# Three stages on one core: the gate's logits as 16 more columns of a product, weights decoded 768 words at a time

## The chip, the cores and the metric

The kernel runs on one core of a Trainium2 chip. The metric is the time of one execution on the device in microseconds (us); the median of three runs before the change is 947.0 us (946.34 to 947.67). The engines: TensorE (PE for its products, PEld for its weight loads), VectorE (DVE), ScalarE (ACT), GpSimd (POOL) and SyncE (SP), which issues nearly all DMAs. Each runs its own instructions in program order and waits for the others by semaphores.

## The reference, cut to what matters

```python
# 1. attention with decay: 4 batches, 8 heads, 768 steps, 48 wide; state is a 48x48 matrix per head
for t in range(S):
    y[:, :, t] = r_t @ (state + (u * k_t) outer v_t)
    state = w_t[:, None] * state + k_t outer v_t
x = y.transpose(0, 2, 1, 3).reshape(3072, 384)
# 2. gated feed-forward, weights given as float64 (384 x 1536, 384 x 1536, 1536 x 384)
xn = x / sqrt(mean(x * x) + 1e-6) * rms_g
x = (silu(xn @ w_gate) * (xn @ w_val)) @ w_out
# 3. eight experts, one per token (384 x 8 gates; 384 x 1024, 1024 x 384 per expert)
logits = x @ w_gate2;  e = argmax(logits);  p = softmax(logits)[e]
out = p * sigmoid(x @ w_output_gate)[e] * (relu(x @ w1[e]) @ w2[e])
```

## The kernel before, in words

The 3072 tokens are 24 tiles of 128 rows, and three tiles make a block of 384. Blocks 0 to 7 run one after the other. In each, TensorE computes the first product (function `l1`) for twelve slices f of 128 hidden columns, 18 matmuls of 384 columns per slice, and two slices later the second product (`l2`), 9 matmuls of 384 columns per slice. Every product is done in parts: an operand is split into a high part in the type fp32r and a low rest, and three products (high by high, high by low, low by high) replace one in full fp32 (`mm3`).

Between these matmuls stand slots, two in `l1` and one after `l2`, 36 and two more in a block. In a slot a table of offsets (`OFFS`, `TGAP`) advances the attention of the three tiles of the next block by a step, and `route` for the tiles of the block before. The attention of tiles 0 to 2 runs ahead of block 0, in an order written out by hand (`START_SEQ`: 0, 1, 2 advance that tile, 9 is a decode step, a negative number issues dummy matmuls). Then eight experts follow in units of 256 to 432 tokens.

Four places matter here.

- **Decoding.** The feed-forward weights arrive as float64 words of 8 bytes. `decode` takes a piece of 128 x 384 words: a load by SP, a conversion of the low half by ACT (line 100), a shift and a mask on DVE (lines 101 and 105), an integer addition on POOL (109), the high part by ACT (112) and the rest on DVE or, for every third piece, on POOL (115). There are 36 pieces. `decode_step` moves three pieces a stage on; the start calls it 8 times, every slot of block 0 once.
- **Scores.** For tiles from 6 on (`PARTED`, line 337) the scores are products in parts: ACT and DVE make high parts and rests of k and r (lines 369 to 400), and TensorE runs twelve matmuls of 256 columns (407). Tiles 0 to 5 use eight fp32 matmuls of 128 columns that contract over 48 rows, alternately in the lower and the upper half of the array (413).
- **Normalization.** Line 459 multiplies a tile of y by its row's factor and by `rms_g` on DVE; then TensorE transposes it (465), ACT takes the high part (467), DVE the rest (468).
- **Routing.** `route` transposes each tile of the feed-forward's result (534), copies it by ACT (538) and multiplies it by the 16 gate columns (527), a tile per step; then DVE finds the expert, TensorE counts places, and POOL scatters the rows to a scratch table in HBM. The last block is routed within the first unit of the first expert.

Buffers come from one ring of 18 slots, PSUM has three banks ("m") for attention, routing and transposes, two ("a") for `l1` and three ("l") for `l2`.

Of the kernel before, what the change touches and what calls it, by code (L numbers as in the profile page):

```python
# [9 lines left out]
F32 = mybir.dt.float32  # L10
# [12 lines left out]
def kernel(  # L23
# [15 lines left out]
    ROUTE_AT=(0, 1, 2, 3, 4),  # L39
    OFFS=((0, 0, 6.7, 7.5, 8.8, 10.5, 11.4, 11.5, 12.7), (0, 1.6, 3.2, 4.8, 6.4, 8, 9.6, 11.2, 12.8, 14.4)),  # L40
    TGAP=(8.9, 9.0),
    START_SEQ=(-11, 0, 0, 0, -4, -4, -6, -4, 0, 9, 1, 0, 1, 9, -4, 0, 1, 1, 2, -4, 0, 0, 1, 2, 0, 9, 1, -4, 2, 9, -6, 1, 2, 1, 2, 9, -4, 1, 2, 9, -2, 2, 2, 9, -6, 2, 9),
# [13 lines left out]
    ZC, LC, IC = DM, DM + 1, DM + 1 + E  # L56
    ROW = DM + 2 + E
# [13 lines left out]
    SLOT = -(-max(1536, SETW) // 8) * 8  # L71
# [3 lines left out]
    ring = ctx.enter_context(tc.tile_pool(name="ring", bufs=18))  # L75
# [4 lines left out]


# [6 lines left out]
    def decode(src, on_pool):  # L88
# [10 lines left out]
        ti, tf = t.bitcast(I32), t.bitcast(F32)  # L99
        nc.scalar.activation(out=low, in_=raw[:, :, 0], func=AF.Copy, scale=2.0 ** -29)  # L100
        nc.vector.tensor_scalar(
            t, raw[:, :, 1], 3, 0x3FFFFFF8, op0=ALU.logical_shift_left, op1=ALU.bitwise_and
# [3 lines left out]
            out=t, in0=raw[:, :, 1], scalar=0xC0000000, in1=t, op0=ALU.bitwise_and,  # L106
# [4 lines left out]
        hi, lo = src[2]()  # L111
        nc.scalar.activation(out=hi, in_=tf, func=AF.Copy)
        yield
# [16 lines left out]
    def split_rows2(raw):  # L130
        t = ring.tile([P, 2, 2 * DM], FR, tag="ring", name="rows2")
        split(raw.rearrange("p c n -> p (c n)"), t)
        return t.rearrange("p s (c n) -> p s c n", c=2)
# [9 lines left out]
    def split_w1(raw):  # L143
        t = ring.tile([P, 2, KD * 2 * P], FR, tag="ring", name="w1s")
        split(raw.rearrange("p c f -> p (c f)"), t)
        return t.rearrange("p s (c f) -> p s c f", c=KD)
# [7 lines left out]
    def ring_view(shape, dtype=F32):  # L154
        t = ring.tile([P, SLOT], dtype, tag="ring", name="rv")
        n = 1
        for x in shape:
            n *= x
        names = "abc"[:len(shape)]
        dims = " ".join(names)  # L160
        return t[:, 0:n].rearrange(f"p ({dims}) -> p {dims}", **dict(zip(names[1:], shape[1:])))


    def constants():
# [23 lines left out]
        c["g"] = const.tile([P, DM], F32, name="g_bc")  # L188
        nc.scalar.dma_start(out=c["g"], in_=rms_g.partition_broadcast(P))
        return c  # L190

    def route_constants(c, const):
# [3 lines left out]
        c["wr"] = const.tile([P, KD, 2 * E], F32, name="wr")  # L196
        nc.sync.dma_start(out=c["wr"], in_=w_gates)

# [62 lines left out]
    PARTED = 6  # L261
# [21 lines left out]
    def load_tile(i):  # L283
# [4 lines left out]
        if i == NSET:  # L288
            t = ring_view([SETW])
# [17 lines left out]
    def load_v(i):  # L307
# [3 lines left out]
        t = p3.tile([P, H, D], F32, tag="v", name="vt")  # L311
# [14 lines left out]
    def attention(c, i, xh, xl, col):  # L326
# [10 lines left out]
        parted = i >= PARTED  # L337
# [51 lines left out]
        if parted:  # L389
            rh, rl = wide  # L390
            kl = sc.tile([P, NPR, P], FR, tag="kl", name="kl")
            nc.vector.tensor_tensor(out=kl, in0=kq, in1=kh.bitcast(F32), op=ALU.subtract)
            for q in range(2):
                pr = slice(64 * q, 64 * q + 64)
                nc.scalar.activation(out=rh[pr, :, q], in_=rq[pr], func=AF.Copy)
            yield
            for q in range(2):
                pr = slice(64 * q, 64 * q + 64)
                nc.vector.tensor_tensor(
# [783 lines left out]
```

## Time and profile before

| | us |
|---|---|
| median of the runs (three) | 947.0 |
| the profiled execution | 944.41 |
| its span, from first to last instruction | 942.7 |
| PE busy, DVE busy, ACT busy, POOL busy | 890.2, 592.3, 326.3, 227.0 |
| mean granted clock of TensorE, 1 is full | 0.968 |

The profiled execution is 2.6 us under the median. A busy PE is not one at its peak: matmuls are pipelined, so a single one is shown as some 0.34 us while the next starts 0.175 us later. What a matmul costs is read from start to start. The span falls into a start (up to 49.6 us), block 0 (to 155.3), blocks 1 to 6 (to 621.0), block 7 (to 681.7) and the experts.

### The profile page before, as it was taken

To read this page: it belongs to the slowest core of one execution; us is meant where nothing else is said; L and a number is where in the kernel's file an instruction comes from. 1 tells how busy PE (TensorE), PEld (TensorE's weight loads), DVE (VectorE), ACT (ScalarE), POOL (GpSimd) and SP (SyncE) were. 2 spreads that over 40 slices of the span, in tenths; PEclk is the share of its full clock that TensorE was granted. 3 is DMA by queue.
4 is the path that set the end of the run, shared out by engine and by line. 5 is a ranking of instruction groups with operands and counts; after the bars stand their busy time and mean duration, and the time that the engine had idled before them with its cause. 6 is when DMAs were issued, how large, how long until landed. Compare 5 with 4: busy or idle time off the path is not lost. (4 is left out here: it accounts for less than half of the span.)

```text
span 942.7 us, 14866 instructions
## 1 busy us (share of the span) xinstructions
PE 890.2 (94%) x5579; PEld 864.3 (92%) x5579; DVE 592.3 (63%) x1147; ACT 326.3 (35%) x672; POOL 227.0 (24%) x326
## 2 busy tenths in 40 slices
PE   7786979999999999999999999999999999999995
PEld 4676979999999999999999998999999999999994
DVE  6899996764675586477367566624447565656551
ACT  1254344331332422333233232333434344434430
POOL 6666553212031031131113103201020100122111
PEclk8787799999999999999999999999999999999998
DMA  9445551761122121023012111101224363454510
GB/s 242 147 139 157 155 167 49 204 184 35 43 77 59 42 77 52 20 76 83 10 43 85 51 43 43 51 1 60 68 79 163 118 204 97 149 176 156 166 54 21
DMA packets 65142, 90.62 MB, mean 96 GB/s; under 512 B 5971, under 2 KB 55875, under 8 KB 65069
## 3 DMA queue, kind: packets, MB, share of 16 engines
q1 hardware_dynamic: 61213, 79.70, 28.7%
q0 software_dynamic: 3568, 9.57, 2.7%
q8 instruction: 44, 0.72, 0.3%
q10 hardware_dynamic: 288, 0.39, 0.1%
q14 instruction: 29, 0.24, 0.1%
HBM read 73.41 MB, written 16.73 MB: 96 GB/s over the span
## 5 line engine op out<-in xcount | busy, mean ns | idle before, releaser
L150 PE MATMUL a<-xh,gv 128*128 128x384 f32 x1152 | 325.7, 348 | 4.0 <-DVE sil L489 2.9
L150 PEld LDWEIGHTS a<-xh,gv 128*128 128x128 f32 x1152 | 215.9, 192 | 5.6 <-DVE sil L489 3.8
L150 PE MATMUL a<-xl,gv 128*128 128x384 f32 x576 | 197.5, 343 | 0.0
L489 DVE TENSOR_TENSOR sil<-a,sil 128x384 f32<-128x384 f32 x96 | 53.2, 554 | 112.5 <-PE a L150 110.6
L150 PE MATMUL a<-xh,w1s 128*128 128x256 f32 (+7 forms) x432 | 111.7, 324 | 1.5 <-DVE hl L868 1.2
L150 PEld LDWEIGHTS a<-xl,gv 128*128 128x128 f32 x576 | 111.0, 193 | 0.4 <-DVE xl L468 0.4
L491 ACT ACTIVATE hh<-sil 128x384 fp32r<-128x384 f32 x96 | 50.4, 525 | 163.1 <-DVE sil L489 163.1
L503 PE MATMUL l<-wo,hh 128*128 128x384 f32 x288 | 101.7, 353 | 0.0
L504 PE MATMUL l<-wo,hh 128*128 128x384 f32 x288 | 98.1, 340 | 0.0
L505 PE MATMUL l<-wo,hl 128*128 128x384 f32 x288 | 98.0, 340 | 0.0
L868 DVE SCALAR_TENSOR_TENSOR hl<-a,hh 128x256 fp32r<-128x256 f32 (+7 forms) x80 | 40.7, 510 | 69.6 <-ACT hh L867 66.0
L230 POOL DMA_INDIRECT out_dram<-row,iu x30 | 34.7, 1156 | 201.4 <-DVE row L879 162.3
L150 PEld LDWEIGHTS a<-xh,w1s 128*128 128x128 f32 x432 | 76.7, 188 | 2.7 <-DVE hl L868 1.6
L487 ACT ACTIVATE sil<-a 128x384 f32<-128x384 f32 x96 | 47.0, 489 | 81.0 <-PE a L150 70.7
L867 ACT ACTIVATE hh<-a 128x256 fp32r<-128x256 f32 (+7 forms) x80 | 36.4, 455 | 96.9 <-PE a L150 92.8
L150 PE MATMUL a<-xl,w1s 128*128 128x256 f32 (+7 forms) x216 | 69.6, 322 | 0.1
L431 PE MATMUL m<-vt,am 128*128 128x48 f32 x384 | 58.3, 281 | 5.9 <-issue 4.7
L150 PE MATMUL l<-rows,hh 128*128 128x384 f32 (+3 forms) x240 | 62.5, 341 | 0.0
L440 POOL TENSOR_SCALAR ss<-ss 128x1 f32<-128x1 f32 x24 | 8.4, 352 | 223.9 <-ACT am L439 223.5
L494 DVE TENSOR_TENSOR hl<-sil,hh 128x384 fp32r<-128x384 f32 x96 | 53.1, 553 | 13.5 <-ACT hh L491 13.0
L431 PEld LDWEIGHTS m<-vt,am 128*128 128x128 f32 x384 | 54.2, 206 | 7.0 <-issue 5.0
L375 POOL TENSOR_TENSOR y<-vt,g 128x384 f32<-128x384 f32 x24 | 23.5, 979 | 132.0 <-PE m L382 73.2
(220 smaller groups left out, 1725.7 us busy)
## 6 DMA issues: line engine op xcount, KB each, us to landing
raw<-in_moe_w_dram SPq DMA_DIRECT2D x64, 384.0 KB, 3.5
rk<-in_rkv_dram SPq DMA_DIRECT2D x24, 384.0 KB, 4.1
set<-in_feat_dram SPq DMA_DIRECT2D x46, 192.0 KB, 3.3
scr<-zrow SPq DMA_DIRECT2D x8, 788.0 KB, 5.1
vt<-in_rkv_dram SPq DMA_DIRECT2D x24, 192.0 KB, 2.3
raw<-in_moe_w_gate_dram SPq DMA_DIRECT2D x12, 384.0 KB, 3.3
raw<-in_moe_w_val_dram SPq DMA_DIRECT2D x12, 384.0 KB, 4.0
raw<-in_moe_w_out_dram SPq DMA_DIRECT2D x12, 384.0 KB, 3.5
```

What stands on the lines that cost most here:

```text
L150: nc.tensor.matmul(o, a, b, start=start and i == 0, stop=stop and i == 2, skip_group_check=True)
L230: ins = nc.gpsimd.indirect_dma_start(out=dst, out_offset=bass.IndirectOffsetOnAxis(ap=idx, axis=0), in_=rows, in_offset=None, bounds_check ...
L431: nc.tensor.matmul(yp[:, 2 * p + q], score, vv[:, 2 * p + q], start=not ch, stop=True, skip_group_check=True,)
L487: nc.scalar.activation(out=sil, in_=o, func=AF.Silu)
L489: nc.vector.tensor_tensor(out=sil, in0=pg[1], in1=sil, op=ALU.mult)
L491: nc.scalar.activation(out=hh, in_=sil, func=AF.Copy)
L494: nc.vector.tensor_tensor(out=hl, in0=sil, in1=hh.bitcast(F32), op=ALU.subtract)
L503: nc.tensor.matmul(o, hh[:, sl], wh, start=f == 0, stop=False)
L504: nc.tensor.matmul(o, hh[:, sl], wl, start=False, stop=False)
L505: nc.tensor.matmul(o, hl[:, sl], wh, start=False, stop=f == KF - 1)
L867: nc.scalar.activation(out=hh, in_=o, func=AF.Relu)
L868: nc.vector.scalar_tensor_tensor(out=hl, in0=o, scalar=0.0, in1=hh.bitcast(F32), op0=ALU.max, op1=ALU.subtract)
```

## The change

What it does:

- `w_out` times the 16 gate columns is formed once, while `w_out` is decoded: per slice three transposes, a copy by ACT, three matmuls of 16 columns, and the split into high part and rest (`route_columns`). The result stands behind the 384 columns of the slice, so that every matmul of `l2` has 400 columns and its result holds the 16 logits. `route` loses its transposes, copies and products and goes from five steps to two. In the first unit of the first expert these come in slots 0 and 1 (before 0 to 4).
- Decoding takes 768 words a piece: 18 pieces, two slices' `w_out` in one, and the converted low half is written over the raw words. The start calls `decode_step` 6 times; block 0's slots call it as before.
- The scores of all tiles are the fp32 matmuls of 128 columns; the products in parts are gone, and a step of the attention with them.
- ACT applies the row's factor to y; `rms_g` is a factor per partition in the splitting after the transposes, in three instructions of 128 columns on ACT and three on DVE.
- The ring becomes 12 slots and 6 wider ones; a few buffers move. The gate columns are loaded at the start by ACT's queue, `rms_g` as a small column in place of 192 KB.

The diff, cut to its core:

```diff
-    def decode(src, on_pool):
-        raw = dec.tile([P, DM, 2], U32, tag="raw64", bufs=3, name="raw64")
-        nc.sync.dma_start(out=src[0](raw), in_=src[1])
-        yield
-        t = dec.tile([P, DM], U32, tag="dt", bufs=4, name="dt")
-        low = dec.tile([P, DM], I32, tag="dl", bufs=2, name="dl")
+    def decode(n, loads, dst, on_pool, more=None):
+        raw = loaded(n)
+        for put, words_in in loads:
+            nc.sync.dma_start(out=put(raw), in_=words_in)
+        yield
+        t = dec.tile([P, 2, DM], U32, tag="dt", bufs=3, name="dt")
+        ti, tf, low = t.bitcast(I32), t.bitcast(F32), raw.bitcast(I32)[:, :, :, 0]
...
         nc.scalar.activation(out=hi, in_=tf, func=AF.Copy)
+        if more:
+            more(tf)
         yield
...
-        if parted:
-            kh = p2.tile([P, NPR, P], FR, tag="kq", name="kh")
-            nc.scalar.activation(out=kh, in_=kq, func=AF.Copy)
...
-            nc.vector.tensor_tensor(out=kl, in0=kq, in1=kh.bitcast(F32), op=ALU.subtract)
...
-                nc.scalar.activation(out=rh[pr, :, q], in_=rq[pr], func=AF.Copy)
-            yield
...
-                nc.vector.tensor_tensor(
-                    out=rl[pr, :, q], in0=rq[pr], in1=rh[pr, :, q].bitcast(F32), op=ALU.subtract
-                )
...
-            if parted:
-                o = ab[p // 2][:, p % 2 * 2:p % 2 * 2 + 2]
-                mm3(o.rearrange("p q t -> p (q t)"), kh[0:64 + D, p], kl[0:64 + D, p],
...
-        nc.vector.scalar_tensor_tensor(
-            out=y2, in0=y2, scalar=ss, in1=c["g"], op0=ALU.mult, op1=ALU.mult
-        )
+        nc.scalar.activation(out=y2, in_=y2, func=AF.Copy, scale=ss)
...
-        nc.scalar.activation(out=xh[:, :, cs], in_=xT, func=AF.Copy)
-        nc.vector.tensor_tensor(
-            out=xl[:, :, cs], in0=xT, in1=xh[:, :, cs].bitcast(F32), op=ALU.subtract
-        )
+        for kk in range(KD):
+            gk = c["g"][:, kk:kk + 1]
+            nc.scalar.activation(out=xh[:, kk, cs], in_=xT[:, kk], func=AF.Copy, scale=gk)
+            nc.vector.scalar_tensor_tensor(
+                out=xl[:, kk, cs], in0=xT[:, kk], scalar=gk, in1=xh[:, kk, cs].bitcast(F32),
+                op0=ALU.mult, op1=ALU.subtract,
+            )
...
+    def route_columns(f, tf):
+        o = bank("m", 3, [P, KD, P])
+        for kk in range(KD):
+            nc.tensor.transpose(o[:, kk], tf[:, kk * P:(kk + 1) * P], c["ident"])
+        wt = turned[:, f % 4] if f < KF - 2 else dec.tile([P, 2, DM], F32, tag="dt", bufs=3, name="wt")[:, 0]
+        wt = wt.rearrange("p (c f) -> p c f", c=KD)
+        nc.scalar.activation(out=wt, in_=o, func=AF.Copy)
+        yield
+        o = bank("m", 3, [P, 2 * E])
+        for kk in range(KD):
+            nc.tensor.matmul(o, wt[:, kk], c["wr"][:, kk], start=kk == 0, stop=kk == KD - 1)
+        t = wo[f // 2]
+        hi, lo = t[:, 0, f % 2, DM:WIDTH], t[:, 1, f % 2, DM:WIDTH]
+        nc.scalar.activation(out=hi, in_=o, func=AF.Copy)
+        nc.vector.tensor_tensor(out=lo, in0=o, in1=hi.bitcast(F32), op=ALU.subtract)
+        yield
...
-        lg = bank("m", 3, [P, nt, 2 * E])
...
-                    nc.tensor.matmul(
-                        lg[:, j - 1], xs[j - 1][:, kk], c["wr"][:, kk], start=kk == 0,
...
-                    nc.tensor.transpose(xp[:, kk], xr[:, j, kk * P:(kk + 1) * P], c["ident"])
...
-                nc.scalar.activation(out=xs[j], in_=xp, func=AF.Copy)
-                yield
...
         def decode_step():
             n = done_w[0]
+            routed_step()
             if n < len(pieces) + LAG:
                 advance(n + 2, 1)
                 advance(n, 2)
...
+                routed_step()
                 done_w[0] += 1
...
-            acc = [bank(f"l{a}", 1, [P, DM]) for a in range(nt)]
+            acc = [bank(f"l{a}", 1, [P, WIDTH]) for a in range(nt)]
...
-                        weights_to(3 * f + 3)
+                        weights_to(f + f // 2 + 1)
```

What stands on the engines, before and after, at three places.

TensorE in a steady block (xh, xl, gv: the first product's operands; wr: the gate columns; rh, rl, kh, kl: parts of the scores' operands; l: the second product). Before:

```order
L150 MATMUL a<-xh,gv 128x384 x2
L150 MATMUL a<-xl,gv 128x384
L150 MATMUL a<-xh,gv 128x384
L527 MATMUL m<-wr,xs 128x16 x3
L150 MATMUL m<-rh,kh 128x256
L150 MATMUL m<-rl,kh 128x256
L150 MATMUL m<-rh,kl 128x256
```

The last three come four times in a row. After:

```order
L515 MATMUL l_2224<-wo,hh 128x400
L516 MATMUL l_2224<-wo,hl 128x400
L403 MATMUL m<-rq,kq 128x128 x8
L165 MATMUL a<-xh,gv 128x384
L165 MATMUL a<-xl,gv 128x384
L165 MATMUL a<-xh,gv 128x384 x2
```

The gate products are out of the block, one row of eight stands for the scores, and the second product is 400 wide.

DVE in block 0 (dt: a piece in work; raw, gv, wo: its source and results; sil, hl: the hidden values; y, m: attention). Before, a little over a slot:

```order
L494 TENSOR_TENSOR hl<-sil,hh 128x384
L101 TENSOR_SCALAR dt<-raw_711 128x384
L115 TENSOR_TENSOR gv<-dt,gv 128x384
L105 SCALAR_TENSOR_TENSOR dt<-raw_711,dt 128x384
L435 TENSOR_TENSOR y<-m,y 128x384
```

After, the same place:

```order
L484 TENSOR_TENSOR wo<-m,wo 128x16
L505 TENSOR_TENSOR hl<-sil,hh 128x384
L114 TENSOR_SCALAR dt<-raw_779 128x768
L130 TENSOR_TENSOR gv<-dt,gv 128x768
L118 SCALAR_TENSOR_TENSOR dt<-raw_779,dt 128x768
L424 TENSOR_TENSOR y<-m,y 128x384
```

A slot holds twice the words, and a short subtraction for the gate columns. The last piece's subtraction (L130) now stands ahead of slice 5's sil, before (L115) ahead of slice 10's.

SP's DMAs in the start (set: w, k, r of a tile; vt: v; rk: r and k by rows; raw: pieces). Before:

```order
L95 DMA raw_124<-in_moe_w_gate_dram 128x3x256
L297 DMA set_81<-in_feat_dram 48x4x128 x2
L299 DMA set_81<-in_feat_dram 48x1024 x2
L95 DMA raw_130<-in_moe_w_val_dram 128x3x256
L312 DMA vt<-in_rkv_dram 128x384
L95 DMA raw_134<-in_moe_w_out_dram 128x768
```

After (rv: a piece in a ring slot):

```order
L109 DMA raw_130<-in_moe_w_gate_dram 128x3x256
L109 DMA raw_130<-in_moe_w_val_dram 128x3x256
L310 DMA set_81<-in_feat_dram 48x4x128 x2
L312 DMA set_81<-in_feat_dram 48x1024 x2
L109 DMA rv<-in_moe_w_gate_dram 128x3x256
L109 DMA rv<-in_moe_w_val_dram 128x3x256
L325 DMA vt<-in_rkv_dram 128x384
L109 DMA raw_141<-in_moe_w_out_dram 128x2x768
```

Three pieces of twice the size go ahead of the loads for tiles 1 and 2.

## Rows read from the trace of the kernel before

**Rows 1.** Stretches: start, block 0, blocks 1 to 6, block 7; busy us (instructions), clock, DMA share.

```profile
0.00:49.60 49.60, 35.65 (x201) 26.42 (x201) 36.55 (x61) 12.39 (x27) 30.07 (x46) 0.79 0.70 195
49.60:155.30 105.70, 87.86 (x482) 84.12 (x483) 98.36 (x153) 45.89 (x98) 60.10 (x71) 0.86 0.45 139
155.30:621.00 465.70, 458.94 (x3007) 453.45 (x3006) 291.84 (x549) 144.29 (x303) 92.92 (x132) 1.00 0.23 66
621.00:681.70 60.70, 60.70 (x366) 60.35 (x364) 24.98 (x52) 21.57 (x41) 3.61 (x6) 1.00 0.15 50
```

**Rows 2.** Timeline of TensorE in block 2: start us, us, instruction, count.

```profile
250.13 0.74 PE L527 MATMUL m<-wr,xs 128*128 128x16 f32 x6
250.72 0.37 PE L150 MATMUL m<-rh,kh 112*128 112x256 f32 x1
...
251.04 0.28 PE L150 MATMUL m<-rh,kl 112*128 112x256 f32 x1
...
252.22 0.34 PE L503 MATMUL l<-wo,hh 128*128 128x384 f32 x1
...
252.75 0.34 PE L503 MATMUL l<-wo,hh 128*128 128x384 f32 x1
...
253.81 0.35 PE L425 MATMUL m<-states,rq 128*128 128x96 f32 x2
...
256.40 0.42 PE L150 MATMUL a<-xh,gv 128*128 128x384 f32 x1
...
259.85 0.93 PE L446 MATMUL m<-vt,kt 128*112 128x96 f32 x8
260.56 0.42 PE L503 MATMUL l<-wo,hh 128*128 128x384 f32 x1
```

**Rows 3.** Timeline of TensorE at the first expert's start, with its idle time in brackets.

```profile
682.68 0.53 PE L534 MATMUL m<-ident,rv 128*128 128x128 f32 x3
682.96 1.31 PE L150 MATMUL a<-rv,w1s 128*128 128x256 f32 x9
...
692.15 0.18 PE L901 MATMUL m<-acc,one_b 128*128 128x8 bf16 x1 [0.53 <-DVE acc L577]
```

**Rows 4.** Waits: who waited for what, us in total, times, longest.

```profile
PE m L150 <- DVE rl L399: 5.7, 6, 1.3
```

**Rows 5.** Timeline of TensorE in block 0, tile 4's score products.

```profile
103.28 1.16 PE L413 MATMUL m<-rq,kq 48*128 48x128 f32 x16 [0.23 <-DVE rq L364]
104.38 0.44 PE L503 MATMUL l<-wo,hh 128*128 128x384 f32 x1
104.66 0.34 PE L504 MATMUL l<-wo,hh 128*128 128x384 f32 x1
```

**Rows 6.** Groups of DVE instructions in block 0: shape, count, busy us, mean ns, idle.

```profile
L101 DVE TENSOR_SCALAR dt<-raw 128x384 uint32<-128x384 uint32 x29 | 22.9, 791 | 0.5 <-DMA raw<-in_moe_w_val_dram 0.5
L105 DVE SCALAR_TENSOR_TENSOR dt<-raw,dt 128x384 uint32<-128x384 uint32 x29 | 18.7, 646 | 0.3
L115 DVE TENSOR_TENSOR gv<-dt,gv 128x384 fp32r<-128x384 f32 x20 | 16.8, 840 | 0.0
L494 DVE TENSOR_TENSOR hl<-sil,hh 128x384 fp32r<-128x384 f32 x12 | 6.6, 549 | 0.6 <-ACT hh L491 0.6
```

**Rows 7.** Groups over the whole span: DVE on 768 words.

```profile
L120 DVE TENSOR_TENSOR w1s<-raw,w1s 128x768 fp32r<-128x768 f32 x32 | 30.5, 953 | 4.5 <-ACT w1s L119 4.0
```

**Rows 8.** Groups of GpSimd (POOL) in block 0.

```profile
L109 POOL TENSOR_TENSOR dt<-dt,dl 128x384 int32<-128x384 int32 x30 | 33.5, 1116 | 31.4 <-DVE dt L105 28.1 <-ACT dl L100 2.1 <-ACT gv L112 1.1
```

**Rows 9.** Timeline of GpSimd: one decode addition in block 0.

```profile
60.32 1.19 POOL L109 TENSOR_TENSOR dt<-dt,dl 128x384 int32<-128x384 int32 x1 [1.30 <-DVE dt L105]
```

**Rows 10.** Timeline of DVE beside that addition.

```profile
60.56 1.16 DVE L101 TENSOR_SCALAR dt<-raw 128x384 uint32<-128x384 uint32 x1
...
74.02 0.35 DVE L101 TENSOR_SCALAR dt<-raw 128x384 uint32<-128x384 uint32 x1
```

**Rows 11.** Timeline of GpSimd in the start.

```profile
23.82 1.00 POOL L351 TENSOR_TENSOR rk<-rk 128x384 f32<-128x384 f32 x1 [7.09 <-DMA rk<-in_rkv_dram]
```

**Rows 12.** Timeline of DVE in the start.

```profile
25.92 0.55 DVE L371 TENSOR_REDUCE g<-rk 128x8 f32<-128x384 f32 x1 [2.99 <-POOL rk L352]
```

More of the change, by code (lines that the diff above doesn't have):

```diff
@@ L79, with slot_of @@
     tabd = dram.tile([P, 4], I32, name="tabd")
+    taken = [0]
+    def slot_of(n, dtype, name, big=None):
+        if big is None:
+            big = taken[0] % 3 == 2
+            taken[0] += 1
+        size = WSLOT if big else SLOT
+        t = ring.tile([P, size], dtype, tag="big" if big else "ring", bufs=6 if big else 12, name=name)
+        return t[:, 0:n]
     def bank(tag, bufs, shape):
@@ L187, in constants @@
         )
-        c["g"] = const.tile([P, DM], F32, name="g_bc")
-        nc.scalar.dma_start(out=c["g"], in_=rms_g.partition_broadcast(P))
+        c["g"] = const.tile([P, KD], F32, name="g_col")
+        nc.scalar.dma_start(out=c["g"], in_=rms_g.rearrange("(c p) -> p c", p=P))
+        c["wr"] = const.tile([P, KD, 2 * E], F32, name="wr")
+        nc.scalar.dma_start(out=c["wr"], in_=w_gates)
         return c
@@ L513, in route @@
         nc.tensor.matmul(b_ps, c["one_b"], c["acc"], start=True, stop=True)
-        base = const.tile([P, E], F32, tag="base", name="base")
+        base = late.tile([P, E], F32, tag="base", name="base")
         if last:
@@ L635 @@
         pads(sets_w[1], (nc.vector, nc.gpsimd))
+        kts = ring_view([NSET + 1, NPR * P], big=False).rearrange("p i (a t) -> p i a t", a=NPR)
         pieces = []
         for f in range(KF):
-            for a, src in enumerate((words(w_gate), words(w_val))):
-                def dst(f=f, a=a):
-                    if a == 0:
-                        gv[f] = ring.tile([P, 2, 2, KD, P], FR, tag="ring", name="gv")
-                    return tuple(gv[f][:, s, a].rearrange("p c f -> p (c f)") for s in range(2))
-                pieces.append((
-                    lambda t: t.rearrange("p (c f) t -> p c (f t)", c=KD),
-                    src[:, 2 * f * P:2 * (f + 1) * P].rearrange("(c p) f -> p c f", p=P), dst,
-                ))
@@ L647, in dst @@
-            def dst(f=f):
-                if f % 2 == 0:
-                    wo[f // 2] = ring.tile([P, 2, 2, DM], FR, tag="ring", name="wo")
-                return tuple(wo[f // 2][:, s, f % 2] for s in range(2))
-            pieces.append((
-                lambda t: t.rearrange("p n t -> p (n t)"), words(w_out)[f * P:(f + 1) * P, :], dst,
-            ))
+            def dst(f=f):
+                gv[f] = ring.tile([P, 2, 2, KD, P], FR, tag="ring", name="gv")
+                return tuple(gv[f][:, s].rearrange("p a c f -> p a (c f)") for s in range(2))
@@ new lines, with dst, more @@
+            pieces.append(([
+                (lambda t, a=a: t[:, a].rearrange("p (c f) t -> p c (f t)", c=KD),
+                 src[:, 2 * f * P:2 * (f + 1) * P].rearrange("(c p) f -> p c f", p=P))
+                for a, src in enumerate((words(w_gate), words(w_val)))
+            ], dst))
+            if f % 2:
+                def dst(f=f):
+                    wo[f // 2] = ring.tile(
+                        [P, 2, 2, WIDTH], FR, tag="big", bufs=6, name="wo"
+                    )
+                    return tuple(wo[f // 2][:, s, :, 0:DM] for s in range(2))
+                def more(tf, f=f):
+                    for i in range(2):
+                        routed[f - 1 + i] = route_columns(f - 1 + i, tf[:, i])
+                pieces.append(([
+                    (lambda t: t.rearrange("p a n t -> p a (n t)"),
+                     words(w_out)[(f - 1) * P:(f + 1) * P, :].rearrange("(a p) n -> p a n", p=P))
+                ], dst, more))
@@ L654, with routed_step, loaded @@
         gens_w = []
         done_w = [0]
+        def routed_step():
+            for g in list(routed.values())[0:1]:
+                if next(g, 1):
+                    del routed[min(routed)]
+        spare = [ring_view([2, DM, 2], U32, False) for _ in range(2)]
+        def loaded(n):
+            if n < 12 and n % 2:
+                return spare[n // 2 % 2]
+            return dec.tile([P, 2, DM, 2], U32, tag="raw64", bufs=2, name="raw64")
         def advance(m, stage):
@@ L691 @@
         load_v(2)
-        kts = ring.tile([P, NSET + 1, NPR, P], F32, tag="ring", name="kts")
         nc.gpsimd.memset(states, 0.0)
```

112 lines of the change are left out of this document (40 added, 72 removed).

## The prediction

> **What bounds the kernel now.** I read the busy time by stretch first, then TensorE's order of time, then the waits. In the stretches [rows 1] the reader is to see two regimes. In blocks 1 to 7 TensorE is busy 458.9 of 465.7 us and 60.7 of 60.7 at a clock of 1.00, and DVE only 63% and 41%: what leaves TensorE's queue there shortens the kernel by its length. In block 0 it is the other way: DVE is busy 98.4 of 105.7 us, TensorE 87.9 at a clock of 0.86. So every part of the change has two prices, one by stretch.
>
> **Blocks 1 to 7, part by part.** A matmul of 384 columns costs 0.177 us from start to start (252.22 to 252.75, three of them), one of 256 columns 0.118 (251.04 to 252.22, ten) [rows 2]. The difference, 0.059 us for 128 columns, makes 0.0072 us for 16.
>
> Gate columns added: 108 matmuls a block, seven blocks, 756 x 0.0072 = +5.4 us. The same 108 in block 0 stand beside a DVE that is late, and cost nothing by themselves. The wider copies out of PSUM add 16 of 384 columns on ACT, which was busy 144 of 466 us [rows 1]; nothing.
>
> Routing removed, per tile: six records for the gate product, 250.13 to 250.72 [rows 2], 0.59 us; three transposes, 682.68 to 682.96 [rows 3], 0.28 us; and the first matmul behind such a group takes 0.26 to 0.28 us instead of 0.18 (104.38 to 104.66 [rows 5] is one), so some 0.1 more. 1.0 us x 21 tiles = -21.0 us in blocks 1 to 7, and -3.0 for the last block's three tiles, in the first expert unit.
>
> Scores, 18 tiles from 6 on: twelve matmuls in parts take 250.72 to 252.22, 1.50 us [rows 2], and TensorE waited 5.7 us in all for their rests [rows 4]. The fp32 form took 103.28 to 104.38, 1.10 us, on tile 4, at full clock, and 0.1 in the matmul behind it [rows 5]. 18 x (1.50 - 1.20) + 5.7 = -11.1 us. Late next would be a product that waits for DVE's other work; that engine has a third of its time free there and loses three instructions a tile, so I give nothing back. Bounds: +0 if the waits return in another place and the form is no cheaper in a dense stretch, -13.
>
> First expert unit: before, the two routing steps that count came in slots 3 and 4 with matmuls of `l2` between; TensorE then idled 0.53 us for the counts [rows 3]. Now the chain of DVE's small operations starts in slot 0, behind the copies out of PSUM, and its count is asked for at the end of slot 1. TensorE must wait for both halves of it. Estimate +2.2 us (between 0 and +4): the wait of rows 3 grows by the matmuls no longer ahead of it, about twelve at 0.177. Behind it stand only that unit's matmuls.
>
> `rms_g`: y's factor goes from DVE to ACT, and the splitting gets two more instructions on each. Both have room in blocks 1 to 7; nothing on the path.
>
> Sum of these: +5.4 - 21.0 - 3.0 - 11.1 + 2.2 = -27.5 us.
>
> **The start and block 0.** Here DVE decides. Its three decode instructions take 0.791, 0.646 and 0.840 us on 384 words in block 0 [rows 6], though the first takes 0.35 when nothing is in its way (74.02 [rows 10]) and a plain subtraction 0.55 [rows 6]. What is in the way is POOL: its addition runs from 60.32 to 61.51 [rows 9], and DVE's next L101, begun at 60.56, ends at 61.72 [rows 10]. Excess over the free durations: 29 x 0.44 + 29 x 0.10 + 20 x 0.29 = 21.4 us, against 33.5 us of POOL additions [rows 8].
>
> With 768 words: a subtraction of that size takes 0.953 us where 384 take 0.549 [rows 6, 7], so a pair saves 0.15; I put L101 at 0.55 by the same step, the other two at 0.953. Free work: 36 x (0.35 + 0.55) + 24 x 0.55 = 45.6 us before, 18 x (0.55 + 0.953) + 12 x 0.953 = 38.5 after, -7.1. The normalization takes 0.3 us a tile off DVE or a little more; twelve short subtractions for the gate columns at some 0.2 add 2.4. If DVE were busy throughout, start and block 0 would so become about 7 us shorter. I don't take that, for two reasons.
>
> First, the density. Slots still call one decode step each, with twice the words, and the last piece now falls in slice 5. So the first five slices hold 13 pieces (L114, L118) and 10 subtractions: 13 x (0.55 + 0.953) + 10 x 0.953 = 29.1 us, gate columns 10 x 0.2 = 2.0, the waits for POOL, whose additions are twice as long: 13 x 0.71 = 9.2 (as many a step as before) to 13 x 1.42 = 18.5, and the other DVE work: 98.4 - 22.9 - 18.7 - 16.8 = 40 us over 36 slots [rows 1, 6], 13 of them, 14.4. That is 55 to 64 us in which TensorE mostly waits. Then seven slices of `l1` and nine of `l2` remain, (126 + 81) x 0.177 = 36.6 us, and tile 5 with most of tile 4 at some 5 us each: score 1.1, 253.81 to 256.40 for the sums, 259.85 to 260.56 for the state [rows 2], two sets of transposes at 0.3. 46 us, and DVE has free time that it can't use. TensorE is ahead by a few matmuls when the dense part ends, so 45. Together 100 to 109, plus up to 4 for raw buffers that come free a step later: block 0 as long as before, 105 +- 5.
>
> Second, the start. The DMA engines are busy 0.70 of it [rows 1], moving 195 GB/s; the row loads of tile 1 come so late that POOL waits 7.09 us for them and DVE 2.99 behind it [rows 11, 12]. Three pieces ahead of them now carry 3 x 384 KB more, `rms_g` 192 KB less: 1.0 MB, 4 to 5 us. Six full steps are twelve old ones where eight stood, four more: 4 x 1.5 = +6 us of DVE, while y's product leaves it three times and DVE's idle time takes up some. I take +5, bounds -1 and +9.
>
> Start and block 0: +5, between -7 and +15. The route columns' transposes and products (36 and 36) fall in the part where TensorE waits and cost nothing while DVE is late; uncovered they would cost 12 x (0.59 + 0.28 + 0.1) = 11.6 us.
>
> **The sum** against the profiled execution: 944.4 - 27.5 + 5 = 921.9. The median of the runs lies 2.6 above that execution, so I predict 924.5 us.
>
> **The rivals.**
>
> *Block 0 pays too.* DVE stays busy to the end because the steps stretch, and the saved words count: 924.5 - 5 - 7 = 912.5 us. For it: DVE's 98.4 of 105.7. Against: the order, in which decoding ends at slice 5.
>
> *The scores gain nothing.* fp32 instructions of 128 columns cost two records each; if records can't run side by side in a dense stretch, each costs what one of the gate product does, 0.59 / 6 = 0.1 us [rows 2]: 16 x 0.1 + 0.1 = 1.7 us a tile, 18 x 0.2 = +3.6 against 1.50, less the waits 5.7: -2.1 for -11.1, so 933.5. Against it stand the sixteen records of rows 5, 0.069 us each. The Trainium skill, "FP8 and Floating Point Precision", TensorE Precision Notes, speaks for it and for more: true fp32 makes four passes through the array. By that, an estimate, 8 x 128 x 4 columns at 0.00046 us are 1.9 us a tile and the term about +2, for 937.6 us; rows 5 disagree, since matmuls in the two halves of the array overlap there.
>
> *Slower: block 0 goes into lockstep.* A `w_out` piece's buffer is free only when TensorE has transposed it, and there are three; DVE's next L114 waits for a transpose that stands behind `l1`'s matmuls, which wait for DVE. If the two engines take turns in the twelve steps of block 0, each step adds a half of `l1`, nine matmuls, at the low of the two clocks (1.2 GHz; twice 0.177): 3.2 us, 12 x 3.2 = +38, 962.5 us. It decides from the point where start and block 0 together pass 155.3 + 27.5 = 183 us. For it: the clock of 0.86 shows that TensorE already idles and slows there. Against: the gates' transposes are issued a step after their piece, and `l1` needs DVE only one slice back.
>
> That the routing work was hidden, so that the change does nothing, is excluded by TensorE's full rows in blocks 1 to 7.
>
> **How the numbers follow.** Forecast 0.55 (its own range 915 to 932), block 0 pays 0.2, scores gain nothing 0.13, lockstep 0.06, the rest between or beyond. The range 907 to 941 leaves out lockstep and the tails, 2 in 10. Within 0.2% (1.9 us, about what a measurement of this kernel can tell from no change) of 947: 0.02; slower 0.07, the lockstep and a little; faster 0.91.
>
> **What would show it.** Right: blocks 1 to 6 last some 73.5 us each instead of 77.6, block 7 about 58.5; TensorE full there; block 0 with DVE full for its first 60 us and about half busy afterwards, TensorE the reverse; the first row loads of tile 1 later by 4 us. Wrong: block 0 ends before 150 us or after 175; score products with more than 1.3 us a tile; gaps of TensorE before other products in blocks 1 to 6; 400 columns that cost over 0.19 us.

## The result, and the profile after

The changed kernel takes 951.84 us (median of 7 runs, 949.68 to 954.14); the kernel before took 946.39 us on the same chip (7 runs). The ratio is 1.0059, 95% interval 1.0041 to 1.0076: slower by 5.5 us, where 924.5 us and 907 to 941 were forecast. The profiled execution has a span of 948.8 us for 942.7.

The busy time by stretch answers to [rows 1] (start and end, length, then busy us of PE, PEld, DVE, ACT and POOL, the granted clock, the DMA share, GB/s); the last two lines divide block 0 at 130.0 us, where DVE's last decode instruction ends:

```profile
0.00:59.70 59.70, 39.42 (x219) 29.36 (x219) 40.53 (x62) 19.14 (x36) 36.09 (x45) 0.78 0.74 202
59.70:180.50 120.80, 97.43 (x572) 92.84 (x573) 86.23 (x123) 48.09 (x95) 52.40 (x49) 0.85 0.34 98
180.50:628.20 447.70, 443.33 (x2917) 429.19 (x2917) 245.85 (x506) 127.09 (x285) 98.77 (x128) 1.00 0.25 69
628.20:686.50 58.30, 58.30 (x337) 57.91 (x337) 24.91 (x52) 20.20 (x38) 3.25 (x6) 1.00 0.16 52
59.70:130.00 70.30, 46.93 (x242) 43.29 (x243) 60.71 (x71) 33.82 (x62) 42.82 (x24) 0.77 0.43 129
130.00:180.50 50.50, 50.50 (x332) 49.55 (x331) 25.52 (x53) 14.27 (x34) 9.58 (x25) 0.97 0.21 55
```

Blocks 1 to 7 gained (447.7 us for 465.7, 58.3 for 60.7), and the start and block 0 lost more: +10.1 and +15.1 us. Read DVE's column in block 0: 86.2 us of work where 98.4 stood before, in a block that is 15 us longer. For 70 us DVE is busy 86% and TensorE 67%; for the last 50 it is the reverse, TensorE is full and DVE idle half of the time. In the kernel before, DVE's last decode instruction ends at 144.6 us, and only 10.6 us of the block are left:

```profile
49.60:144.60 95.00, 78.33 (x428) 74.88 (x429) 92.62 (x137) 42.73 (x92) 57.32 (x54) 0.84 0.48 148
144.60:155.20 10.60, 9.43 (x56) 9.13 (x55) 5.68 (x18) 3.06 (x7) 2.69 (x18) 1.00 0.17 55
```

The waits of TensorE in block 0 of the changed kernel (who waits for what: us in total, times, longest) are two lines:

```profile
PE m L472 <- POOL dt L122: 16.2, 5, 5.2
PE m L480 <- ACT rv L476: 7.2, 4, 3.2
```

L472 are the transposes of the route columns, L480 their products. They look like the whole loss. But TensorE waited in block 0 of the kernel before as well, 18.4 us in all, mostly at three other places (y before its transposes, the scores' operand, the first product):

```profile
PE m L465 <- DVE y L459: 8.4, 3, 4.9
PE m L413 <- DVE rq L364: 5.8, 3, 3.1
PE a L150 <- DVE sil L489: 2.4, 2, 2.2
```

So the waits have grown by only 5 us, and TensorE's busy time by 9.6 (97.4 for 87.9), the columns' own work in it. The runs below show that the columns are not the whole loss.

DVE's groups in block 0 answer to [rows 6], POOL's two rows of the start to [rows 11], DVE's one to [rows 12]:

```profile
L114 DVE TENSOR_SCALAR dt<-raw 128x768 uint32<-128x768 uint32 x9 | 12.2, 1357 | 0.6 <-POOL wo L130 0.6
L130 DVE TENSOR_TENSOR gv<-dt,gv 128x768 fp32r<-128x768 f32 x10 | 11.7, 1172 | 0.0
L118 DVE SCALAR_TENSOR_TENSOR dt<-raw,dt 128x768 uint32<-128x768 uint32 x9 | 10.1, 1119 | 0.1
```

```profile
27.99 0.99 POOL L363 TENSOR_TENSOR rk<-rk 128x384 f32<-128x384 f32 x1 [9.82 <-DMA rk<-in_rkv_dram]
29.06 0.99 POOL L364 TENSOR_TENSOR rk<-rk,u_bc 128x384 f32<-128x384 f32 x1
```

```profile
30.08 0.55 DVE L380 TENSOR_REDUCE g<-rk 128x8 f32<-128x384 f32 x1 [6.55 <-POOL rk L364]
```

Tile 1's rows come 4.2 us later than before (27.99 for 23.82). In block 2, a tile's scores and the second products of a slice (start us, us, count):

```profile
267.71 1.16 PE L403 MATMUL m<-rq,kq 48*128 48x128 f32 x16
268.80 0.44 PE L165 MATMUL a<-xh,gv 128*128 128x384 f32 x1
...
280.28 0.34 PE L514 MATMUL l<-wo,hh 128*128 128x400 f32 x1
...
281.74 0.35 PE L516 MATMUL l<-wo,hl 128*128 128x400 f32 x1
282.38 0.55 PE L453 MATMUL m<-ident,y 128*128 128x128 f32 x3 [0.29 <-ACT y L449]
```

The scores take 267.71 to 268.80, 1.09 us; 400 columns take (281.74 - 280.28) / 8 = 0.183 us. Both were forecast. From the start of the last product to the transposes L453 are 0.64 us, where 0.18 is the pace of the products: TensorE waits for the scaling of y, which the list of steps now sets one slot ahead of them (slots 11 and 12), because the attention has nine steps and the list still has ten times. Before, with ten steps, the two stood two slots apart (12 and 14).

### The profile page after: what moved, and what is told of

Its sections match the earlier page's. It is cut to its first block, busy times and chain, and to the rows that moved or that the text cites. A ratio compares the mean times of both kernels' runs of the same rounds, so it can differ in the third digit from the quotient of the medians.

```text
span 948.8 us, 14645 instructions
## 1 busy us (share of the span) xinstructions
PE 884.6 (93%) x5543; PEld 848.5 (89%) x5543; DVE 537.9 (57%) x1073; ACT 315.5 (33%) x654; POOL 230.9 (24%) x298
## 5 line engine op out<-in xcount | busy, mean ns | idle before, releaser
L514 PE MATMUL l<-wo,hh 128*128 128x400 f32 x288 | 102.5, 356 | 0.0
L515 PE MATMUL l<-wo,hh 128*128 128x400 f32 x288 | 100.0, 347 | 0.0
L516 PE MATMUL l<-wo,hl 128*128 128x400 f32 x288 | 99.5, 345 | 0.0
L505 DVE TENSOR_TENSOR hl<-sil,hh 128x384 fp32r<-128x384 f32 x96 | 54.1, 563 | 33.7 <-ACT hh L502 33.7
L420 PE MATMUL m<-vt,am 128*128 128x48 f32 x368 | 55.1, 278 | 4.5 <-DVE am L407 4.5
L420 PEld LDWEIGHTS m<-vt,am 128*128 128x128 f32 x368 | 51.2, 204 | 5.2 <-DVE am L407 5.0
L516 PEld LDWEIGHTS l<-wo,hl 128*128 128x128 f32 x288 | 54.9, 191 | 0.2
```

Of the source, the lines that this page charges most:

```text
L420: nc.tensor.matmul(yp[:, 2 * p + q], am[q][:, p], vv[:, 2 * p + q], start=not ch, stop=True, skip_group_check=True,)
L505: nc.vector.tensor_tensor(out=hl, in0=sil, in1=hh.bitcast(F32), op=ALU.subtract)
L514: nc.tensor.matmul(o, hh[:, sl], wh, start=f == 0, stop=False)
L515: nc.tensor.matmul(o, hh[:, sl], wl, start=False, stop=False)
L516: nc.tensor.matmul(o, hl[:, sl], wh, start=False, stop=f == KF - 1)
```

## The experiments

Stretches in us of each profiled execution (start: to the first block product; then to the first of the next block); times are medians, ratios against the kernel before on the same chip. Its median lies between 944.6 and 946.4 us on the five chips used, so that times of different rows compare to within 2 us. "..." stands for the kernel with three edits; the last row has the later products too. The two kernels without columns and the one without the factor route their tokens by other logits than the reference's: of these three the stretches are to be read, and no time is given for the first two.

| kernel | start | block 0 | blocks 1–6 | time | ratio (95%) |
|---|---|---|---|---|---|
| before | 49.6 | 105.6 | 465.9 | 946.4 | |
| changed | 59.7 | 120.8 | 447.7 | 951.8 | 1.0059 (1.0041–1.0076) |
| spacing | 59.7 | 120.6 | 442.7 | 947.1 | 1.0021 (1.0010–1.0032) |
| no columns | 55.2 | 117.3 | 447.4 | – | |
| late columns | 60.6 | 127.4 | 447.7 | 956.3 | 1.0101 (1.0078–1.0124) |
| half pace | 59.9 | 109.4 | 447.7 | 939.2 | 0.9939 (0.9921–0.9958) |
| before, double pace | 49.1 | 121.9 | 466.2 | 962.5 | 1.0177 (1.0159–1.0194) |
| before, unparted | 48.7 | 107.4 | 464.4 | 943.9 | 0.9977 (0.9962–0.9992) |
| before, unparted, spaced | 48.8 | 107.8 | 459.5 | 937.7 | 0.9924 (0.9907–0.9941) |
| three edits | 56.1 | 110.7 | 442.7 | 932.7 | 0.9870 (0.9844–0.9897) |
| ... + four steps | 50.0 | 119.0 | 442.7 | 934.1 | 0.9878 (0.9858–0.9898) |
| ... no columns | 51.7 | 106.5 | 442.3 | – | |
| ... + one pair, no factor | 54.2 | 110.0 | 439.7 | 925.8 | 0.9794 (0.9768–0.9821) |
| ... + products later | 51.5 | 112.5 | 442.3 | 929.9 | 0.9845 (0.9827–0.9862) |
| ... + one pair, factor in place | 57.7 | 107.4 | 439.8 | 927.3 | 0.9816 (0.9800–0.9833) |

**Spacing.** The tenth time in the list goes to the ninth step.

```diff
-    (0, 1.6, 3.2, 4.8, 6.4, 8, 9.6, 11.2, 12.8, 14.4)
+    (0, 1.6, 3.2, 4.8, 6.4, 8, 9.6, 11.2, 14.4)
```

> Nine steps are spaced again: the scaling of y and the transposes of a tile stand three slots apart instead of one; nothing else. Theory S: in blocks 1 to 6 TensorE waits 0.3 to 0.46 us at each of 18 tiles' transposes because the scaling on ScalarE is only one slot ahead; the six blocks fall from 447.7 to about 441 us and the total by 6 to 7 us, to about 945. Rival: the wait covers another lateness (the sums or the power that make the scale are themselves late), it only moves to the next products, and the total changes by less than 2 us.

Blocks 1 to 6 fell by 5.0 us, the time by 4.7 (4.2 with each kernel taken against the one before on its chip). Theory S holds, a little smaller than set. The groups of the transposes in blocks 1 to 6, changed kernel and then this one (count, busy us, mean ns, idle us):

```profile
L453 PE MATMUL m<-ident,y 128*128 128x128 f32 x54 | 9.8, 291 | 4.4 <-ACT y L449 3.3
```

```profile
L453 PE MATMUL m<-ident,y 128*128 128x128 f32 x54 | 8.8, 272 | 0.0
```

**No columns.**

```diff
-                    for i in range(2):
-                        routed[f - 1 + i] = route_columns(f - 1 + i, tf[:, i])
+                    nc.scalar.activation(out=hi, in_=tf[:, :, 0:2 * E], func=AF.Copy)
+                    nc.vector.tensor_tensor(out=lo, in0=tf[:, :, 0:2 * E], in1=hi.bitcast(F32), op=ALU.subtract)
```

> Leaves out the forming of the 16 route columns (their transposes, copies and products); the first 16 columns of w_out stand in their place, so the routing and with it the experts' stage are not those of the reference: only the start, block 0 and blocks 1 to 6 are to be read. Theory L (TensorE's queue stands at the columns): of 180.5 us to the end of block 0, the 23 us of waits at the columns' transposes and products go and some of their own 11 us: 155 to 165 us. Rival D (decoding in pieces of 768 words is itself late, whatever TensorE does): TensorE waits in the same places at the next product that needs a weight, 174 to 181 us. Blocks 1 to 6 as in the changed kernel, 447 us, by both.

Block 0 ended at 172.5 us: theory L falls, though D's 174 is not quite reached. Without the columns' work (six short pairs on ACT and DVE stand in for it, 1.3 and 2.7 us) 8.0 us of the 25.3 lost came back: 4.5 in the start, 3.5 in block 0. TensorE's waits of block 0 in this run:

```profile
PE a L165 <- DVE sil L500: 11.3, 3, 5.4
PE m L453 <- ACT y L449: 11.1, 1, 11.1
PE m L403 <- DVE rq L376: 5.9, 2, 4.7
```

The 23 us at the columns became 28 us at three other products, those at which the kernel before waits too. The columns stood first in TensorE's queue behind something that was late anyway.

**Late columns.** They are taken from the stored halves of `w_out`, three decoding steps later.

```diff
-                nc.tensor.transpose(o[:, kk], tf[:, kk * P:(kk + 1) * P], c["ident"])
+            for s in range(2):
+                nc.tensor.matmul(o[:, kk], wo[f // 2][:, s, f % 2, kk * P:(kk + 1) * P], c["ident_r"], start=s == 0, stop=s == 1)
...
+                if done_w[0] < since[f]:
+                    continue
```

> The columns are formed from the stored halves of w_out (6 one-pass products with the identity for 3 transposes) at least three decoding steps after the piece's turn instead of at once; all else as in the changed kernel. Theory L: TensorE no longer meets an unfinished piece, its waits at the transposes (16.2 us) and most of those at the products (7.2 us) go; end of block 0 at 160 to 168 instead of 180.5 us, total 932 to 940. Rival D: end of block 0 at 176 to 182 us, total 947 to 953.

Both missed: block 0 ended at 188.0 us (in an execution 3 us above this kernel's median) and the time rose by 4.4. TensorE's wait for POOL at the transposes was gone, and still 9.3 us of waits for ACT's copy stood at the products; 36 more products came on top. This speaks against theory L a second time, though less clearly, since the edit adds work of its own.

**Half pace.**

```diff
                 plan.step()
-                decode_step()
+                if j or plan.slot % 2:
+                    decode_step()
```

> In block 0 only every second slot decodes a piece, so that the decoding is spread over about two thirds of the block instead of its first half. Theory L: twice the products stand ahead of each piece's columns in TensorE's queue, the piece is then done when TensorE gets there; the end of block 0 falls from 180.5 to 163 to 170 us, total 935 to 942. Rival D: the pieces' own chain is what is late; spread out it still delays each product that needs the weight, 176 us or more, and the total stays within 3 us or gets worse.

Block 0 fell to 109.4 us and the time to 939.2, within L's numbers and against D's; but L had fallen with the run without columns, and here too TensorE waits 14.3 us at the columns (23.4 in the changed kernel). What both had missed is the pace itself, theory P below: a slot decoded one piece before and after, and a piece is now 768 words. Block 0 of this run, whole and divided where DVE's last decode instruction ends:

```profile
59.90:169.30 109.40, 93.25 (x572) 89.28 (x573) 84.22 (x123) 47.31 (x95) 51.94 (x49) 0.90 0.36 108
59.90:147.70 87.80, 71.66 (x423) 68.10 (x424) 74.67 (x98) 41.05 (x79) 47.20 (x30) 0.88 0.40 120
147.70:169.30 21.60, 21.60 (x151) 21.18 (x150) 9.55 (x26) 6.26 (x16) 4.73 (x20) 1.00 0.22 63
```

Behind the decoding 21.6 us are left instead of 50.5, with DVE idle for 12 us instead of 25, and TensorE ahead of that point is busy 82% instead of 67%, at a clock of 0.88 instead of 0.77.

**Before, double pace.** The pace alone, in the kernel without the change: `decode_step()` twice in each slot.

> The kernel before with two decoding steps of 384 words in each slot of block 0 instead of one: as many words per slot as the changed kernel decodes, in pieces of the old size, with no route columns and no other part of the change. Theory P (pace: too many words per slot, so that VectorE and GpSimd set the time of the block's first part and stand idle in its last): block 0 grows from 105.6 to 113 to 121 us, total 953 to 962. Rival G (grain: it is the length of a single 768-word instruction that holds the others up): block 0 at 103 to 109 us, total within 3 us of before.

Block 0 grew by 16.3 us to 121.9, a little past P's range; G falls. So a block 0 as long as the changed kernel's comes about without any of the change. (That the two agree to 1 us is partly chance: the changed one holds 3.5 us of columns as well.) It is divided here, as above, where DVE's last decode instruction ends; then TensorE's waits in it:

```profile
49.10:128.40 79.30, 48.18 (x207) 44.27 (x208) 76.42 (x108) 36.18 (x76) 51.81 (x47) 0.74 0.49 150
128.40:171.00 42.60, 41.46 (x276) 40.01 (x276) 23.80 (x46) 10.14 (x23) 7.72 (x23) 0.98 0.25 65
```

```profile
PE a L150 <- DVE sil L489: 10.4, 4, 2.9
PE m L465 <- DVE y L459: 8.8, 1, 8.8
PE m L413 <- DVE rq L364: 5.8, 2, 4.7
```

DVE is busy 76.4 of the 79.3 us of decoding and 23.8 of the 42.6 behind it. The waits are the three of the run without columns: the first product, whose bank DVE must have read for sil; y before its transposes; the scores' operand. DVE's decoding stands ahead of these in its queue.

**Before, unparted.** `PARTED = 6` becomes `PARTED = NT`.

> The kernel before with the scores of all tiles as one-pass-less plain products (no halves from tile 6 on): the part of the change on the scores alone. The prediction's term: -11.1 us in blocks 1 to 6 (1.20 us per tile for 1.50, and 5.7 us of waits), so 454 to 455 us for 465.9, total about 935. Rival: the plain products cost what the pages on precision suggest, four passes; the six blocks stay within 2 us of 465.9.

Only 1.5 us in the six blocks, 1.8 us in all. By TensorE's start-to-start times the score products fell from 33.8 to 23.3 us, by 10.5, near the term's 11.1; the matmul before the transposes of y (L505) rose from 37.8 to 43.6, since without the parted step these kernels, too, have nine steps on ten times.

**Before, unparted, spaced.** The same with the nine times of the first experiment.

> The kernel before with unparted scores, as in the last run of that kind, and its nine steps spaced again so that the scaling of y stands three slots ahead of the transposes. Theory S: the -10.4 us that the scores' own rows gave were handed back at the transposes (+5.8 us behind L505) and the products around them; with the spacing the six blocks come to 454 to 456 us for 465.9, total 933 to 936. Rival: something else in the blocks takes what the scores give (460 to 465 us, total 941 to 945).

6.4 us in the six blocks, between the two ranges: of the scores' 10.1 us, the spacing holds 5 that were handed back, and 3.7 stay lost in amounts near 1 us over several rows (the route transposes 6.5 for 5.4, for one). Nor do all tiles have the new price here: the scores of twelve take 1.09 us, those of the six that stand right behind `route`'s transposes 1.62 to 1.80. In the changed kernel, which has no such transposes, all eighteen take 1.09.

**Three edits.** Spacing, half pace, and `advance(2, 1)` deleted ahead of tile 2's loads, on the changed kernel.

> The changed kernel with three edits: nine steps spaced again, decoding in every second slot of block 0, and the third piece's load left to the first decoding step instead of ahead of tile 2's. If the parts add up: blocks 1 to 6 at 442.7 us (as alone), block 0 at 109 us (as alone), and the start from 59.7 to 55 to 57 us, since 0.8 MB less stands ahead of tile 1's rows in the DMA queue (their wait ended at 28.0 us, at 23.8 before); total 930 to 932. Rival for the load: the piece comes later to the second part of the start, which loses what the first gains; start 59 to 60 us, total 934.

932.7 us, 0.7 above the forecast. Tile 1's second row product started at 25.88 us for 29.06, and the start fell by 3.8 us against half pace alone; block 0 gave 1.3 back; blocks 1 to 6 take 442.7 us, as alone. The parts add up.

**Four steps in the start.** Two of the six 9s are deleted from the order of the start.

> As the kernel with three edits, and two of the six decoding steps of the start left to block 0 (four pieces of 768 words, where the kernel before took eight of 384). Theory P holds for the start too: its chains on ScalarE and VectorE wait for less decoding, 3 to 5 us less start, block 0 at most 2 us more; total 926 to 930. Rival: the start is bound by the tiles' own chain and the DMA; the two steps only move into block 0, which grows by 3 us or more; total within 2 us of the kernel with three edits.

The rival is right. With as many words in the start as before (4 x 768 = 8 x 384) the start is 50.0 us, as before; the two steps' work costs block 0 8.3 us, more than the 6.1 that the start gains, and the time does not gain.

**Three edits, no columns.** The edit of the second run on this kernel.

> As the kernel with three edits, with the forming of the route columns left out (the first 16 columns of w_out stand for them, so the experts' stage is not to be read). What the columns still cost to the end of block 0 (166.9 us with them). Theory L': with the pace halved the waits at their products (7.1 us in block 0, 5.5 us in the start) and transposes (2.7 us) are on the path: end of block 0 at 150 to 155 us. Rival: they cost about what they cost at the full pace, 8 us: 158 to 160 us.

Block 0 ends at 158.2 for 166.9 us: 8.7 us, the rival's number, again about half in the start (4.4) and half in block 0. The columns have a price of 8 to 9 us at either pace.

**One pair, no factor.**

```diff
-        for kk in range(KD):
-            gk = c["g"][:, kk:kk + 1]
-            nc.scalar.activation(out=xh[:, kk, cs], in_=xT[:, kk], func=AF.Copy, scale=gk)
-            nc.vector.scalar_tensor_tensor(out=xl[:, kk, cs], ...
+        nc.scalar.activation(out=xh[:, :, cs], in_=xT, func=AF.Copy)
+        nc.vector.tensor_tensor(out=xl[:, :, cs], in0=xT, in1=xh[:, :, cs].bitcast(F32), op=ALU.subtract)
```

> As the kernel with three edits, with xh and xl written by one instruction each per tile, as in the kernel before, instead of three pairs that wait for each other; leaves out the factor rms_g. Theory: the chain of three pairs took 1.85 to 2.3 us per tile in the start against some 1.0 for one pair, three times on the path: start 53 to 54 us for 56.1, total 929 to 931. Rival: other work covers it, total within 1.5 us of the kernel with three edits.

6.9 us by the medians, 5.9 with each kernel taken against the one before on its chip; by stretches, which are what counts here, 2.7 to the end of block 0 and, not expected, 3.0 in blocks 1 to 6. In the changed kernel's start the pairs alternate, each waiting for the other engine (ACT's L457 for DVE's L458 of the piece before):

```profile
37.55 0.37 ACT L457 ACTIVATE xh<-m,g_col 128x128 fp32r<-128x128 f32 x1 [3.73 <-DVE xl L458]
37.95 0.35 DVE L458 SCALAR_TENSOR_TENSOR xl<-m,g_col,xh 128x128 fp32r<-128x128 f32 x1 [0.43 <-ACT xh L457]
38.33 0.37 ACT L457 ACTIVATE xh<-m,g_col 128x128 fp32r<-128x128 f32 x1 [0.42 <-DVE xl L458]
38.73 0.35 DVE L458 SCALAR_TENSOR_TENSOR xl<-m,g_col,xh 128x128 fp32r<-128x128 f32 x1 [0.43 <-ACT xh L457]
```

The edit takes away both the alternation and four of six instructions; which of the two it is that costs, this run does not tell.

**Products later.** One more `yield` between a column's transposes and its product, one less behind it.

> As the kernel with three edits, with each column product one step of the route work later behind its transposes, so that ScalarE's copy of them has half a decoding step more. Theory L': TensorE's waits at the products (7.1 us in block 0, 5.5 us in the start) go, 4 to 8 us off the end of block 0 (159 to 163 us for 166.9), total 925 to 929. Rival: ScalarE's and VectorE's own queues set the pace there and the waits move to the next products; total within 2 us of the kernel with three edits.

The start gave 4.6 us, block 0 took 1.8 back: 2.9 us in all (1.8 with each kernel taken against the one before on its chip), 929.9: below L's gain and beyond the rival's, at least by the medians.

**One pair, factor in place.** The last kernel, and in it the three pairs become one pair behind a DVE multiplication of the whole transposed tile.

```diff
+        nc.vector.tensor_tensor(out=xT, in0=xT, in1=c["g"].unsqueeze(2).to_broadcast([P, KD, P]), op=ALU.mult)
```

> As the kernel with three edits and the products later, with rms_g multiplied into the transposed tile by one VectorE instruction in PSUM, and xh and xl then written by one instruction each; nothing is left out. Theory W (the three pairs cost by waiting for each other): most of the 6.9 us that the run with one pair and no factor gained stays, less up to 2 us for the added 128x384 multiplication on the start's path: total 924 to 927. Rival M (it was the factor's own work that cost): the multiplication takes the gain back, total within 1.5 us of 929.9.

927.3 us, between the two theories. In blocks 1 to 6 W holds against M: 439.8 us for 442.3, with the factor's work still done. To the end of block 0 nothing is gained (165.1 for 164.0), so there it stays open how much of the 2.7 us was the pairs and how much the factor. Another 1.4 us of the profiled execution's gain are in the experts' stage, which the edit does not touch: the granted clock did not fall there this time (last section). This version computes all that the reference does and is faster than both kernels: 17.7 us below the one before.

## Why the prediction was wrong

**The step that failed** is "block 0 as long as before, 105 +- 5", and with it start and block 0 at +5. They came to +25.3 us. Removing one thing after the other from the changed kernel, the end of block 0 goes 180.5 (changed), 169.3 (half pace), 166.9 (load left to its step), 158.2 (no columns); less the 2.7 us of one pair without the factor, measured beside the columns and taken to add, 155.5. Before it was 155.2. By stretches, the start's +10.1 are columns 4.4, load 3.8 and pairs 1.9, and block 0's +15.1 are pace 11.4, columns 4.2 and pairs 0.7, less 1.3 from the load. (These are prices in this order of removal.) So:

- **The pace, 11.2 us.** It was in the text: "slots still call one decode step each, with twice the words", and the dense part and the tail were drawn. DVE's work in the dense part came as computed (60.7 us, 55 to 64), and the tail nearly (50.5 us, 46). The error was to let the dense part last as long as DVE's work in it. It lasted 70.3, for DVE idled 9.6 us in it, most of it for ACT's copy of the columns and for the sums of y, the two lines below. The tail came out 4.5 us longer. Doubling the pace in the kernel before, with nothing else changed, costs 16.3 us, and halving it in the changed kernel gives 11.4 back: that shows the cause.

```profile
DVE wo L484 <- ACT wo L483: 4.0, 3, 2.6
DVE y L424 <- PE m L420: 3.2, 1, 3.2
```

- **The columns, 8.7 us for 0.** "Cost nothing while DVE is late" left out the other engines: each column passes through TensorE, ACT, TensorE, ACT and DVE, in queues that other work shares. And half of the price falls in the start, where the text put none. The uncovered price of the text, 11.6 us, was nearer.
- **The load order**: 4 to 5 us were forecast at tile 1's rows and 4.2 came. With the piece's load deferred, 3.8 us of the start returned, less 1.3 in block 0. The other term of the start, +6 us for four more old steps, held too: with two full steps fewer the start is 6.1 us shorter. What failed is the +5 taken for both together, on the ground that idle time takes up some; the start became 10.1 us longer. (The two steps carry some of the columns' work, so these prices overlap with those above.)
- **The pairs, 2.7 us for 0**, in part open, as said.

The lockstep rival had its place right (transposes that wait for a piece) and its cause wrong: without the transposes TensorE waited elsewhere. Its 183 us were not reached. Two of the text's own signs of being wrong came: block 0 ended after 175 us, and TensorE had gaps before other products (L453) in blocks 1 to 6.

**Blocks 1 to 7 and the first expert unit** were set at -27.5 us and came to (948.8 - 180.5) - (942.7 - 155.2) = -19.2. Blocks 1 to 6 gave -18.2 where their terms make -24.4, block 7 -2.3 for -2.2, and the experts, from their first product on, became 1.3 us longer (262.4 for 261.1) where -0.8 was forecast.

In blocks 1 to 6 two steps failed. "I give nothing back", in the scores' term: a tenth step that vanishes changes the distances of all that follow, and y's scaling one slot ahead of the transposes cost 5.0 us. It is not ACT's scaling that does it: unparted, the kernel before, where DVE scales, lost 4.9 (464.4 and 459.5). And "`rms_g` ... nothing on the path": the three pairs cost 3.0. Together these are 8.0 us, more than the 6.2 missing, for the routing, below, gave more than its term. Where the steps are spaced again, the six blocks take 442.7 us, 73.8 each; that 73.5 were forecast is near only because these errors offset each other.

- Gate columns: 0.183 us for 400 columns, 0.184 forecast. Right.
- Scores: 1.09 us, 1.10 forecast. The price is right and the rival's prices, 1.7 us and with four passes 1.9, are out. The term was too large all the same: alone it gave 1.5 us, spaced 6.4, for 11.1.
- Routing: not run alone. Between the kernel before, unparted and spaced, and the changed one, spaced, lie 459.5 - 442.7 = 16.8 us in six blocks, where the terms give 18 tiles x 1.0 - 648 x 0.0072 = 13.3. Of the excess 2.5 us are the scores' (23.7 us to 21.2, start to start): they no longer stand behind `route`'s transposes.
- The first expert's waits. [rows 3] shows one of 0.53 us in the kernel before; the other is the first line here, and the two lines behind it are the changed kernel's:

```profile
690.21 0.19 PE L560 MATMUL m<-oh,tri 128*128 128x24 bf16 x1 [0.23 <-DVE oh L553]
```

```profile
689.99 0.19 PE L552 MATMUL m<-oh,tri 128*128 128x24 bf16 x1 [1.16 <-DVE oh L544]
...
692.00 0.18 PE L907 MATMUL m<-acc,one_b 128*128 128x8 bf16 x1 [1.76 <-DVE acc L569]
```

1.16 + 1.76 - 0.23 - 0.53 = 2.2 us, 2.2 forecast. The wait is right, and still the experts lost 2.1 us against the forecast: behind the second wait the granted clock fell. The 5 us that follow it, changed kernel and then before:

```profile
692.00:697.00 5.00, 5.00 (x26) 5.00 (x27) 2.04 (x9) 0.38 (x1) 3.14 (x6) 0.66 0.33 121
```

```profile
692.10:697.00 4.90, 4.85 (x35) 4.85 (x36) 3.63 (x20) 2.36 (x5) 3.14 (x6) 1.00 0.34 123
```

## What to carry to other kernels

When a piece of background work grows, its rate per slot grows with it. Here halving the calls gave 11.4 us back in block 0; at the full rate the helpers bound the first part of the stretch and stood half idle in the last. The wait that a profile shows names the first instruction in an in-order queue, which need not be the culprit; leave that instruction out once, and see whether the wait moves. And hold a list of waits against the same list of the kernel before: here 23.4 us stood against 18.4. When a step leaves a list of due times, set the others anew: two steps in neighbouring slots here cost half of what a cheaper product gave.

## What was not expected of the hardware

A DVE decode instruction on 768 words in block 0 took 1.357, 1.119 and 1.172 us in the groups shown, for 0.791, 0.646 and 0.840 on 384 [rows 6]. With the pieces that lie in ring slots (tile rv; 1.471 us for the first, 1.322 for the second) the means are 1.385 and 1.182, so the longer form saves 9 to 30% per word, with POOL's additions beside it in both kernels.

The granted clock went with the gaps: 0.77 on the mean, between the levels of 1.2 and 2.4 GHz, over the 70 us in which TensorE was busy 67%, and 0.97 in the 50 us behind, in which it was full; with the pace halved the first 88 us have 0.88 at 82% busy. What part of the pace's 11.4 us is clock, no run here tells; an estimate from the mean clocks of the whole block is 120.8 x 0.15 - 109.4 x 0.10 = 7.2 us if TensorE had worked all the time, so at most that.

In the first expert unit the clock fell to 0.66 on the mean behind two waits of 1.16 and 1.76 us. In the last kernel of the table TensorE waited 1.16 and 1.75 us at the same two places, and its clock stayed at 1.00:

```profile
668.60:673.60 5.00, 4.96 (x36) 4.96 (x37) 2.37 (x10) 0.77 (x2) 3.15 (x6) 1.00 0.33 121
```

The same 30 products ran in 5.85 us in the changed kernel (692.04 to 697.89) and in 4.32 at the full clock (668.68 to 673.00), so that 1.5 of the experts' 2.1 us are clock. Waits of one length may bring the fall or not; what decides is not shown here.
